# A linear-attention and expert kernel: ids and biases later, first weights copied to a fixed buffer

## The chip, the cores and the metric

The kernel runs on one core of a Trainium2 chip. The core has a matrix engine (TensorE, PE in the profile, with its weight loads shown as PEld), VectorE (DVE), ScalarE (ACT), GpSimd (POOL) and SyncE (SP), which here only issues DMA transfers. Each engine works through its own list of instructions in order; semaphores hold an instruction until what it needs is there. The metric is the device time of one execution in microseconds, the median of the runs.

## The reference

Two stages in a row, cut to what matters:

```python
# 1. gated linear attention, B=4, H=8, S=768, D=48
scale = np.minimum(mag, 0.999) / (mag + 1e-06)      # mag = |a|, a = a_re + i a_im
for t in range(S):
    S_re, S_im = (ar * S_re - ai * S_im + kv, ar * S_im + ai * S_re)   # kv = k_t outer v_t
    y[:, :, t] = q_t @ S_re
# 2. a mixture of experts on x = y as (3072 tokens, 384), top 1 of E=8, F=1024
logits = x @ w_gate + modality_bias[modality_id]
e_idx = argmax(logits); gate_w = softmax(logits)[e_idx]
out[mask] = gate_w[mask, None] * (relu(x[mask] @ w1[e]) @ w2[e])       # for each expert e
```

The ids (`modality_id`) and the bias table are needed only for the logits of the second stage.

## The kernel before

The attention is done in 24 *units* of 128 time steps by 1 batch, two units to a *pair* (x = 0 to 11). For a pair, `load_a`, `load_qk` and `load_v` fetch the inputs, `logs` and `quotients` turn the gates into logarithms and angles (L367 squares on ACT, L368 their sum on DVE, L369 and L370 products and signs, L373 logarithm, L394 and L395 on DVE again), `moduli` and `fractions` sum them along time with matmuls, `waves` takes sine and cosine, and `unit` does the rest: L513 and L520 scale and rotate q and k on DVE, L528 transposes on PE, then the products (L538, L548, L575, L582), the state (L560, L562, L567, L568, with the decay that goes out to memory and back through L425 and L430), and L596, which gives the token's row and its logits at once. The first pair is treated in two halves. All input loads are issued by SP, in one order.

The second stage first chooses experts (`route`) and scatters each token's row to a slot in memory (L718, POOL). The kernel is written for tokens that use two of the eight experts: `weights` loads the w1 and w2 of these two into slots 0 and 1 (`w1s` takes over the buffers of `ab`, `w2s` those of `cs`). Thirteen expert tiles follow, seven early ones (`start_e`, `slot_e`) whose tokens come from the first 16 units, and six late ones; all have 256 tokens but the last, which has 128. A tile is: load of x (L899, SP), 6 transposes (L911), copy (L917, ACT), up in two halves of 12 matmuls (L939) each followed by a relu (L946, ACT), down in two blocks of 8 matmuls (L953), scaling (L961, L963) and a scatter to the output (L968). Which of the two slots a tile uses is known only when the kernel runs: it is read from `slot` into a register of PE (`number`, L876), and the weights are addressed through it.

The order of instructions on PE, ACT, DVE and SP is not written by hand: `Plan.solve` runs through time with an estimated duration for each step and gives a free engine the ready step with the lowest rank. `land` and `queue` are its estimates of a DMA's latency and of its time in the DMA queue; a step without `queue` is taken to land without standing behind other loads. It also gives out buffers: `PM` (2 of them) holds `pm` in the units. The engines then keep this order, whatever the real times are.

Of the kernel before, what the change touches and what calls it, by code (L numbers as in the profile page):

```python
# [12 lines left out]
BF16 = mybir.dt.bfloat16  # L13
# [5 lines left out]
ET = mybir.EngineType  # L19
# [156 lines left out]
class Kernel:  # L176
# [432 lines left out]
    def setup(self):  # L609

        P, nc = self.P, self.nc
        r = self.rp = self.pool("rp", 2)
        nM = self.m_bias.shape[0]
        mb = r.tile([128, nM, E_], F32, name="mb", bufs=1)
        ids = r.tile([128, self.G, self.B, 2], I32, name="ids", bufs=1)

        def loads():
            for u in range(2):
                nc.sync.dma_start(out=self.sel[u * HALF:u * HALF + self.D, :, self.D:], in_=self.w_gate.rearrange("(j u d) e -> u d j e", u=2, d=self.D)[u])
            nc.sync.dma_start(out=mb[:].rearrange("p m e -> p (m e)"), in_=self.m_bias.rearrange("m e -> (m e)")[None, :].broadcast_to([128, nM * E_]))  # L620
            for b in range(self.B):
                nc.sync.dma_start(out=ids[:, :, b], in_=self.ids[b * self.G * L:(b + 1) * self.G * L].bitcast(I32).rearrange("(g p w) -> p g w", p=L, w=2))

        P.step(SP, 0.7, loads, writes=[("sel",), ("ids",)], rank=30.0, land=3.0)

        def biases():
            is_m = r.tile([128, self.NU], F32, name="is_m", bufs=1)
            one = r.tile([128, self.NU, E_], F32, name="one_m", bufs=1)
            for m in range(nM):
                nc.vector.tensor_scalar(is_m[:], ids[:].rearrange("p g b w -> p (g b) w")[:, :, 0], float(m), None, Alu.is_equal)  # L630
# [10 lines left out]
    def route(self, m0, m1, rank):  # L641

        P, nc, r = self.P, self.nc, self.rp
        n, M = m1 - m0, 8
# [23 lines left out]
            box.update(sh=sh, oneh=oneh, acc=acc[:])  # L668
            self.acc.append(acc[:])

        P.step(DVE, 1.3, choose, reads=[("bias",), *[("lg", m) for m in range(m0, m1)], *([("acc",)] if m0 else [])], writes=[("acc",), ("oneh", key), ("sh", key)], rank=rank)

        def ranks():
            before = self.acc[self.batches.index((m0, m1)) - 1] if m0 else None
# [36 lines left out]
            box["pos"] = t("pos_i", dt=I32, bufs=3)  # L711
            nc.vector.tensor_copy(box["pos"], pos)

        P.step(DVE, 0.8, slots, reads=[("rank", key), ("place",), ("oneh", key)], writes=[("pos", key)], rank=rank + 2)
        for m in range(m0, m1):
            def scatter(m=m):
                lo = self.raw["LO", "all"]
# [18 lines left out]
    def guess(self, rank):  # L736

        P, nc = self.P, self.nc
        P.tile(("cnt", 0), "bank")
        P.step(PE, 0.2, lambda: self.count("cnt", 0), reads=[("acc",)], writes=[("cnt", 0)], rank=rank)  # L740
        self.ab = ab = self.small("ab", 2, E_)
        row = self.small("place_row", 2, E_)
        self.place = self.keep.tile([128, 2 * E_], F32, name="place")
        io8 = self.iota[0:1, 0:E_]

        def choose():
            used, nth, nab, two, tw = self.small("used", E_), self.small("nth", E_), self.small("nab", E_), self.small("two", 2, E_), self.small("tw", 2)
# [12 lines left out]
            nc.vector.scalar_tensor_tensor(row[:, 1], ab[:, 1], float(self.N - 1), row[:, 1], Alu.mult, Alu.add)  # L760

        P.step(DVE, 2.0, choose, reads=[("cnt", 0)], writes=[("first",), ("prow",)], rank=rank + 1)
# [22 lines left out]
    def early(self, rank):  # L785

        P, nc, N = self.P, self.nc, self.N
        P.tile(("cnt", "e"), "bank")
        P.step(PE, 0.2, lambda: self.count("cnt", "e"), reads=[("acc",)], writes=[("cnt", "e")], rank=rank)
        self.eA = self.small("eA", 1)  # L790

        def places():
            c2, c, is_b, st = self.small("c2e", 2), self.small("ce", 1), self.small("isb_e", NE), self.small("st_e", NE)
            self.counts_of_two("e", c2)
            f = self.floor_shift("fe", c2[:, 0:1], 8)
            nc.vector.tensor_scalar(self.eA[:], f[:], float(NE), None, Alu.min)
# [9 lines left out]
        P.step(DVE, 2.0, places, reads=[("cnt", "e")], writes=[("early",)], rank=rank + 1)  # L806

    def final(self, rank):

# [32 lines left out]
        P.step(DVE, 3.2, places, reads=[("cnt", "f"), ("early",)], writes=[("final",)], rank=rank + 1)  # L842

        def masks(ps):
            at = self.rp.tile([128, NF_, 2], F32, name="at_f", bufs=1)
# [32 lines left out]
    def expert(self, n, rank):  # L878
# [34 lines left out]
        def xT():  # L913
            return self.buf(("xT", n), KD, m * 128, dt=BF16)
# [13 lines left out]
                nc.vector.tensor_tensor(self.meta[:, n, 0:m].bitcast(I32), meta.bitcast(I32), self.pen[:, i, 0:m], Alu.bitwise_or)  # L928

        P.step(DVE, 0.15, kept, reads=[("xg", n), *([] if early else [("pen",)])], writes=[("meta", n)], rank=rank + 1.5)  # L930
        for q in range(2):
            def up(q=q):
                if q == 0:
                    box["slot"] = bass.ds(self.number(slot[0:1, i:i + 1], ET.PE, 1), 1)
                hp = self.pair((f"h{q}", n), 2, m * 128)
                for f in range(4):
                    ff = 4 * q + f
                    for k in range(KD):
                        nc.tensor.matmul(hp[:, f // 2, f % 2], self.w1s[:, box["slot"], k, ff * 128:(ff + 1) * 128].rearrange("p s f -> p (s f)"), xT()[:, k], start=k == 0, stop=k == KD - 1)  # L939

            P.step(PE, 0.65 * m, up, reads=[("xT", n), known, ("w1", 0), ("w1", 1)], writes=[(f"h{q}", n)], rank=rank + 2)
            eng = ACT

            def relu(q=q):
                to = hT()[:, 4 * q:4 * q + 4].rearrange("p (b f) n -> p b f n", b=2)
                nc.scalar.activation(to, self.pair((f"h{q}", n), 2, m * 128), Act.Relu)  # L946

            P.step(eng, 0.45 * m + 0.05, relu, reads=[(f"h{q}", n)], writes=[("hT", n, q)], rank=rank + 2)
        for s in range(m):
            def down(s=s):  # L950
                yp = self.pair(("yps", n), Dt)[:, s]
                for f in range(NF):
                    nc.tensor.matmul(yp, hT()[:, f, s * 128:(s + 1) * 128], self.w2s[:, box["slot"], f].rearrange("p s d -> p (s d)"), start=f == 0, stop=f == NF - 1)  # L953
# [232 lines left out]
```

## Time and profile before

| | |
|---|---|
| median of 3 runs | 392.07 us (389.61 to 392.19) |
| the profiled execution | 391.36 us, span 389.7 us |
| PE busy | 310.8 us (80%) |
| ACT busy | 246.4 us (63%) |
| DVE busy | 215.1 us (55%) |
| POOL busy | 63.7 us (16%) |
| L939 on PE | 312 matmuls, 70.7 us |
| L953 on PE | 200 matmuls, 36.8 us |

All durations in the profile are from the one profiled execution. A busy row has, in this order, the line in the code, engine, operation, output and inputs by the program's names, shape and count; behind the bar the busy time in us, the mean of one in ns, and behind the next bar the idle time just before it with what ended it. In rows in order of time the first two numbers are start and duration in us, and a bracket shows the idle time before. `PEldq` and `SPq` are the instruction queues of PE and SP; FUSED_REGOPS is an instruction that computes an address in registers.

### The profile page before, as it was taken

Reading aid. Unit: us, or ns where it says so; the run is one execution under the profiler, and the core shown is the slowest. Engines: PE = TensorE matmul, PEld = TensorE weight load, DVE = VectorE, ACT = ScalarE, POOL = GpSimd, SP = SyncE. Lnnn points to the kernel's source line nnn. Section 1 sums busy time; section 2 is a strip of 40 time slices with the busy share of each in tenths; the row PEclk is TensorE's granted clock in tenths of the full one; section 3 lists DMA queues with packets and bytes.
Section 4 is the critical chain, followed back from the end, with each engine's and each line's share of the span. In section 5 each row is a group of like instructions: output and inputs, shape, how many; then the busy total and the mean of one; then the engine's idle time right before and its main releaser. Section 6 shows DMA issues by size and latency. Waiting matters only on the chain.

```text
span 389.7 us, 14470 instructions
## 1 busy us (share of the span) xinstructions
PE 310.8 (80%) x5990; PEld 210.1 (54%) x5990; DVE 215.1 (55%) x431; ACT 246.4 (63%) x297; POOL 63.7 (16%) x93
## 2 busy tenths in 40 slices
PE   0006483788999899999996979899999999999980
PEld 0002362665767668686776667785645454454530
DVE  1026586669998999999997699830351010000000
ACT  4007694999999999898996797752524333434310
POOL 8000000000000027005002210030253141222220
PEclk9999998699999999999999799999999999999986
DMA  8986335446696727774698249430132130311110
GB/s 164 206 99 110 69 72 82 83 85 112 113 177 103 121 55 155 140 133 108 116 172 142 70 75 207 70 87 2 62 105 82 41 116 15 115 40 53 40 45 7
DMA packets 153965, 37.50 MB, mean 96 GB/s; under 512 B 145938, under 2 KB 151592, under 8 KB 153896
## 3 DMA queue, kind: packets, MB, share of 16 engines
q1 hardware_dynamic: 148264, 26.26, 37.6%
q0 software_dynamic: 5632, 10.25, 10.2%
q8 instruction: 52, 0.85, 0.9%
q14 instruction: 17, 0.14, 0.1%
HBM read 32.47 MB, written 7.33 MB: 102 GB/s over the span
## 4 chain that ended last, share of the span: by engine, by line
PE 54%; issue 14%; DVE 11%; ACT 7%; SPq 6%; DMA 3%; POOL 2%; POOLq 0%; DVEq 0%; ACTq 0%
PE ps L939 11%; PE ps L953 6%; PE ps L582 5%; PE ps L548 5%; PE ps L458 5%; PE ps L538 5%; PE ps L528 4%; PE ps L410 3%; PE ps L575 3%; PE ps L596 3%; POOL out_dram L968 2%; DVE qk L520 2%; PE ps L463 2%; ACT qt L532 2%; DVE cs L474 1%
## 5 line engine op out<-in xcount | busy, mean ns | idle before, releaser
L939 PE MATMUL ps<-neg,ab 128*128 128x256 bf16 (+1 forms) x312 | 70.7, 265 | 3.7 <-issue 2.1
L946 ACT ACTIVATE qi<-ps 128x1024 bf16<-128x1024 f32 (+1 forms) x26 | 25.8, 990 | 69.5 <-PE ps L939 56.0
L718 POOL DMA_INDIRECT x_slots<-lo,pos_i x24 | 27.5, 1147 | 183.5 <-DVE lg L605 146.0
L939 PEld LDWEIGHTS <-ab 128*128 x312 | 29.7, 96 | 43.8 <-issue 10.7
L410 PE MATMUL ps<-lm,half 128*128 128x384 f32 x48 | 23.6, 577 | 31.1 <-DVE lm L394 29.6
L528 PE MATMUL ps<-ident,qk 64*128 64x64 f32 x768 | 33.5, 238 | 14.9 <-DVE qk L520 13.2
L520 DVE TENSOR_TENSOR qk<-cs,qi 128x1536 f32<-128x1536 f32 x24 | 41.7, 1751 | 3.0 <-ACT cs L487 2.9
L963 DVE TENSOR_SCALAR lm<-ps,meta 128x384 f32<-128x384 f32 x12 | 7.4, 616 | 63.1 <-PE ps L953 63.1
L968 POOL DMA_INDIRECT out_dram<-lm,meta x25 | 24.6, 985 | 89.5 <-ACT lm L961 84.4
L528 PEld LDWEIGHTS ps<-ident,qk 64*128 64x128 f32 x768 | 28.7, 149 | 18.6 <-DVE qk L520 8.5
L953 PE MATMUL ps<-cs,qi 128*128 x200 | 36.8, 333 | 0.5 <-ACT qi L946 0.5
L313 ACT ACT_TABLE_LOAD x27 | 34.6, 1283 | 1.4 <-PEq L1170 0.9
L373 ACT ACTIVATE sq<-sq 128x1536 f32<-128x1536 f32 (+1 forms) x13 | 18.2, 1398 | 21.0 <-DVE sq L368 21.0
L548 PE MATMUL ps<-v,qk 64*64 64x48 f32 x1408 | 29.3, 228 | 2.2 <-ACT kt L532 1.4
L538 PE MATMUL ps<-qt,kt 128*64 128x64 f32 x768 | 28.1, 225 | 2.9 <-issue 1.6
L548 PEld LDWEIGHTS ps<-v,qk 64*64 64x64 f32 x1408 | 26.3, 142 | 4.4 <-ACT kt L532 1.6
L410 PEld LDWEIGHTS ps<-lm,half 128*128 128x128 f32 x48 | 9.0, 216 | 35.3 <-issue 32.1
L538 PEld LDWEIGHTS ps<-qt,kt 128*64 128x64 f32 x768 | 24.7, 138 | 5.3 <-ACT qt L532 2.3
L458 PE MATMUL ps<-tan,turn 128*128 128x384 f32 x48 | 22.1, 543 | 6.3 <-ACT tan L441 4.8
L953 PEld LDWEIGHTS <-qi 128*128 128x128 bf16 x200 | 19.3, 99 | 13.5 <-ACT qi L946 1.9
L532 ACT COPY kt<-ps 128x1024 f32<-128x1024 f32 x24 | 24.4, 1016 | 1.9 <-PE ps L528 1.6
L532 ACT COPY qt<-ps 128x1024 f32<-128x1024 f32 x24 | 24.6, 1027 | 1.1 <-PE ps L528 1.1
(166 smaller groups left out, 509.2 us busy)
## 6 DMA issues: line engine op xcount, KB each, us to landing
ab<-in_a_re_dram SPq DMA_DIRECT2D x24, 192.0 KB
ab<-in_a_im_dram SPq DMA_DIRECT2D x24, 192.0 KB
qi<-in_k_dram SPq DMA_DIRECT2D x24, 192.0 KB
qi<-in_q_dram SPq DMA_DIRECT2D x24, 192.0 KB
v<-in_v_dram SPq DMA_DIRECT2D x24, 192.0 KB
tan<-x_slots SPq DMA_DIRECT2D x12, 194.0 KB
ab<-in_moe_w_dram POOLq DMA_DIRECT2D x2, 768.0 KB, 8.1
cs<-in_moe_w_dram POOLq DMA_DIRECT2D x2, 768.0 KB, 12.0
```

The costliest lines, as they stand in the source:

```text
L313: self.P.step(ACT, 1.3, lambda: nc.scalar.preload_act_table_set(which), writes=[("table",)], rank=self.rank_table)
L410: nc.tensor.matmul(ls[:, i], self.half[:], lm, start=True, stop=False)
L458: nc.tensor.matmul(us[:, i], self.turn[:], self.buf(("tan", x), 2, H, D)[:, i], start=True, stop=False)
L520: nc.vector.tensor_tensor(self.buf(("QK", w), 4 * H, HALF)[:, :, 0:D], wave, twice, Alu.mult)
L528: nc.tensor.transpose(tp[:, s, h], QK()[rows_[s], k, h].rearrange("t c d -> t (c d)"), self.ident[rows_[s], rows_[s]])
L532: P.step(ACT, 0.91, lambda name=name, to=to: nc.scalar.copy(self.buf((to, w), 2, H, HALF), self.pair((name, w), H, HALF)), reads=[(name, w ...
L538: nc.tensor.matmul(wp[rows_[s], h, :], KT[:, s, h], QT[:, s, h], start=True, stop=True)
L548: nc.tensor.matmul(up[c * HALF:(c + 1) * HALF, s, h], QK()[rows_[s], 0, h, c], V[rows_[s], h, 0:D], start=True, stop=True)
L718: put = nc.gpsimd.indirect_dma_start(out=self.xs, out_offset=bass.IndirectOffsetOnAxis(ap=box["pos"][:, m - m0:m - m0 + 1].bitcast(U32), a ...
L939: nc.tensor.matmul(hp[:, f // 2, f % 2], self.w1s[:, box["slot"], k, ff * 128:(ff + 1) * 128].rearrange("p s f -> p (s f)"), xT()[:, k], s ...
L953: nc.tensor.matmul(yp, hT()[:, f, s * 128:(s + 1) * 128], self.w2s[:, box["slot"], f].rearrange("p s d -> p (s d)"), start=f == 0, stop=f ...
L968: sc = nc.gpsimd.indirect_dma_start(out=self.out, out_offset=bass.IndirectOffsetOnAxis(ap=self.meta[:, n, s, 1:2], axis=0), in_=self.buf(( ...
```

## The change

It has four parts. The ids and the bias table are loaded in a step of their own, with a condition, a later rank and a queue time for the planner; the gate weights are loaded in another. The step that makes the biases gets a later rank. For every expert tile a new DVE step (`picked`) reads the slot into a register of DVE and copies the tile's w1 (128 partitions by 3072 bf16) to a buffer of kind `PM`, from which up's matmuls load their weights without a register; the register on PE is now read in down. And some DVE durations that the planner uses are larger.

```diff
-        def loads():
+        def gate():
             for u in range(2):
                 nc.sync.dma_start(out=self.sel[...], in_=self.w_gate...)
+
+        P.step(SP, 0.2, gate, writes=[("sel",)], rank=6.0, land=2.5, queue=0.6)
+
+        def loads():
             nc.sync.dma_start(out=mb..., in_=self.m_bias...)
             for b in range(self.B):
                 nc.sync.dma_start(out=ids[:, :, b], in_=self.ids...)
-        P.step(SP, 0.7, loads, writes=[("sel",), ("ids",)], rank=30.0, land=3.0)
+        P.step(SP, 0.5, loads, reads=[("asked", 2, 1)], writes=[("ids",)], rank=60.0, land=4.0, queue=6.0)
...
-        P.step(DVE, 1.2, biases, reads=[("ids",)], writes=[("bias",)], rank=60.0)
+        P.step(DVE, 1.4, biases, reads=[("ids",)], writes=[("bias",)], rank=90.0)
...
-        P.step(DVE, 1.3, choose, reads=[("bias",), ...
+        P.step(DVE, 1.6, choose, reads=[("bias",), ...
...
-        for name, kind in (("xg", "TAN"), ("xT", "NEG"), ("hT", "QI"), ("y", "LM")):
+        for name, kind in (("xg", "TAN"), ("xT", "NEG"), ("hT", "QI"), ("y", "LM"), ("w1t", "PM")):
             P.tile((name, n), kind)
...
+        def w1t():
+            return self.buf(("w1t", n), KD, self.F, dt=BF16)
+
+        def picked():
+            at = bass.ds(self.number(slot[0:1, i:i + 1], ET.DVE, 1), 1)
+            nc.vector.tensor_copy(w1t()[:, None], self.w1s[:, at])
+
+        P.step(DVE, 0.95, picked, reads=[known, ("w1", 0), ("w1", 1)], writes=[("w1t", n)], rank=rank + 1.5)
         for q in range(2):
             def up(q=q):
-                if q == 0:
-                    box["slot"] = bass.ds(self.number(slot[0:1, i:i + 1], ET.PE, 1), 1)
                 hp = self.pair((f"h{q}", n), 2, m * 128)
...
-                        nc.tensor.matmul(hp[:, f // 2, f % 2], self.w1s[:, box["slot"], k, ff * 128:(ff + 1) * 128]..., xT()[:, k], ...)
-            P.step(PE, 0.65 * m, up, reads=[("xT", n), known, ("w1", 0), ("w1", 1)], writes=[(f"h{q}", n)], rank=rank + 2)
+                        nc.tensor.matmul(hp[:, f // 2, f % 2], w1t()[:, k, ff * 128:(ff + 1) * 128], xT()[:, k], ...)
+            P.step(PE, 0.69 * m, up, reads=[("xT", n), ("w1t", n)], writes=[(f"h{q}", n)], rank=rank + 2)
...
             def down(s=s):
+                if s == 0:
+                    box["slot"] = bass.ds(self.number(slot[0:1, i:i + 1], ET.PE, 1), 1)
```

Three places show how the lists of instructions move; from the changed `up` on, the line numbers are up to 12 higher.

The start of DVE's list. `is_m`, `one_m` and `bias` belong to the bias step. Before:

```order
L369 TENSOR_TENSOR tan_60<-ab 128x384
L370 TENSOR_SCALAR neg_62<-ab 128x384
L368 TENSOR_TENSOR sq_59<-sq_59 128x384
L630 TENSOR_SCALAR is_m<-ids 128x24
L632 TENSOR_TENSOR bias<-is_m,mb 128x192
L630 TENSOR_SCALAR is_m<-ids 128x24
L632 TENSOR_TENSOR one_m<-is_m,mb 128x192
L634 TENSOR_TENSOR bias<-bias,one_m 128x192
L369 TENSOR_TENSOR tan_60<-ab 128x384
L370 TENSOR_SCALAR neg_62<-ab 128x384
L368 TENSOR_TENSOR sq_59<-sq_59 128x384
```

And now:

```order
L369 TENSOR_TENSOR tan_60<-ab 128x384
L370 TENSOR_SCALAR neg_62<-ab 128x384
L368 TENSOR_TENSOR sq_59<-sq_59 128x384
L369 TENSOR_TENSOR tan_60<-ab 128x384
L370 TENSOR_SCALAR neg_62<-ab 128x384
L394 TENSOR_SCALAR lm_64<-sq_59 128x384
L368 TENSOR_TENSOR sq_59<-sq_59 128x384
```

The five bias instructions are gone from between the two halves of the first pair. They now stand thirty places later in DVE's list, behind the second unit's L562. SP's list keeps the place of the ids among the opening loads; only the gate weights move ahead of two loads of v.

PE's list at the first expert tile, where `ab` holds w1 and `neg` the tile's transposed x. Before:

```order
L876 TENSOR_LOAD slot_e
L939 ISA
L939 LDWEIGHTS ab
L939 ISA
L939 MATMUL ps<-neg_62,ab 128x256
L939 ISA
L939 LDWEIGHTS ab
L939 ISA
L939 MATMUL ps<-neg_62,ab 128x256
```

And now, with `pm` as the fixed buffer:

```order
L949 LDWEIGHTS pm_70
L949 MATMUL ps<-neg_62,pm_70 128x256
L949 LDWEIGHTS pm_70
L949 MATMUL ps<-neg_62,pm_70 128x256
L949 LDWEIGHTS pm_70
L949 MATMUL ps<-neg_62,pm_70 128x256
```

Of four instructions for each matmul, the two ISA (register) instructions are gone, and the slot's load with them.

DVE's list at the first two copies, among the last units (`mid`, `w` and `lg` are the units' own):

```order
L560 TENSOR_TENSOR mid_90<-st_92,ps 128x384
L880 TENSOR_LOAD slot_e
L940 ISA
L940 COPY pm_70<-ab 128x3072
L930 COPY meta<-tan_60 128x4
L560 TENSOR_TENSOR mid_89<-st_93,ps 128x384
L880 TENSOR_LOAD slot_e
L940 ISA
L940 COPY pm_71<-ab 128x3072
L930 COPY meta<-tan_61 128x4
L541 TENSOR_TENSOR w_87<-ps,mask_128 128x512
```

Before, the same rows stood there without the slot loads and the copies, and all later copies are new rows of the same kind, one for each tile.

More of the change, by code (lines that the diff above doesn't have):

```diff
@@ L669, in choose @@
             self.acc.append(acc[:])
-        P.step(DVE, 1.3, choose, reads=[("bias",), *[("lg", m) for m in range(m0, m1)], *([("acc",)] if m0 else [])], writes=[("acc",), ("oneh", key), ("sh", key)], rank=rank)
+        P.step(DVE, 1.6, choose, reads=[("bias",), *[("lg", m) for m in range(m0, m1)], *([("acc",)] if m0 else [])], writes=[("acc",), ("oneh", key), ("sh", key)], rank=rank)
         def ranks():
@@ L712, in slots @@
             nc.vector.tensor_copy(box["pos"], pos)
-        P.step(DVE, 0.8, slots, reads=[("rank", key), ("place",), ("oneh", key)], writes=[("pos", key)], rank=rank + 2)
+        P.step(DVE, 0.95, slots, reads=[("rank", key), ("place",), ("oneh", key)], writes=[("pos", key)], rank=rank + 2)
         for m in range(m0, m1):
@@ L760, in choose @@
             nc.vector.scalar_tensor_tensor(row[:, 1], ab[:, 1], float(self.N - 1), row[:, 1], Alu.mult, Alu.add)
-        P.step(DVE, 2.0, choose, reads=[("cnt", 0)], writes=[("first",), ("prow",)], rank=rank + 1)
+        P.step(DVE, 2.6, choose, reads=[("cnt", 0)], writes=[("first",), ("prow",)], rank=rank + 1)
         self.spread("place", lambda: row[:].rearrange("o a e -> o (a e)"), 2 * E_, [("prow",)], rank + 2, lambda ps: nc.vector.tensor_copy(self.place[:], ps), [("place",)])
@@ L804, in places @@
             nc.vector.tensor_copy(self.slot_e[:], is_b[:])
-        P.step(DVE, 2.0, places, reads=[("cnt", "e")], writes=[("early",)], rank=rank + 1)
+        P.step(DVE, 2.8, places, reads=[("cnt", "e")], writes=[("early",)], rank=rank + 1)
     def final(self, rank):
@@ L840, in places @@
             nc.vector.tensor_copy(self.others[:], left[:])
-        P.step(DVE, 3.2, places, reads=[("cnt", "f"), ("early",)], writes=[("final",)], rank=rank + 1)
+        P.step(DVE, 5.0, places, reads=[("cnt", "f"), ("early",)], writes=[("final",)], rank=rank + 1)
         def masks(ps):
@@ L938, in up @@
                     for k in range(KD):
-                        nc.tensor.matmul(hp[:, f // 2, f % 2], self.w1s[:, box["slot"], k, ff * 128:(ff + 1) * 128].rearrange("p s f -> p (s f)"), xT()[:, k], start=k == 0, stop=k == KD - 1)
-            P.step(PE, 0.65 * m, up, reads=[("xT", n), known, ("w1", 0), ("w1", 1)], writes=[(f"h{q}", n)], rank=rank + 2)
+                        nc.tensor.matmul(hp[:, f // 2, f % 2], w1t()[:, k, ff * 128:(ff + 1) * 128], xT()[:, k], start=k == 0, stop=k == KD - 1)
+            P.step(PE, 0.69 * m, up, reads=[("xT", n), ("w1t", n)], writes=[(f"h{q}", n)], rank=rank + 2)
             eng = ACT
```

## The prediction

> **What bounds the kernel now.** I read the busy slices first, then each end of the span by itself, because the slices show three regimes.
>
> ```profile
> PE   0006483788999899999996979899999999999980
> DVE  1026586669998999999997699830351010000000
> ACT  4007694999999999898996797752524333434310
> 0.00:20.00 20.00, 0.00 (x0) 0.00 (x0) 1.42 (x3) 4.62 (x6) 8.10 (x40) 1.00 1.01 186
> 320.00:340.00 20.00, 19.60 (x105) 9.40 (x103) 1.53 (x4) 7.57 (x9) 4.62 (x5) 1.00 0.24 78
> ```
>
> A slice is 9.7 us. Until about 80 us the engines have gaps; from 80 to 260 us PE, DVE and ACT are all full; after that PE alone is full. The last two rows are from the table of stages (PE, weight loads, DVE, ACT, POOL, then granted clock, DMA share, GB/s): in the first 20 us DVE works 1.42 us while the DMA engines are saturated at 186 GB/s, and in a late stage PE works 19.60 of 20 us while DVE works 1.53. So the first and the last stage have one limit each, and the change touches both.
>
> The start, from DVE's and ACT's waits up to 60 us and the timeline:
>
> ```profile
> DVE is_m L630 <- DMA ids<-in_moe_modality_id_dram: 20.1, 1, 20.1
> ACT sq L373 <- DVE sq L368: 21.0, 2, 20.4
> 5.76 0.56 DVE L368 TENSOR_TENSOR sq<-sq 128x384 f32<-128x384 f32 x1
> 7.10 0.83 ACT L367 ACTIVATE sq<-ab 128x768 f32<-128x768 f32 x1
> 21.90 2.40 SPq L622 DMA_DIRECT2D ids<-in_moe_modality_id_dram  x4
> 26.40 0.18 DVE L630 TENSOR_SCALAR is_m<-ids 128x24 f32<-128x24 int32 x1 [20.08 <-DMA ids<-in_moe_modality_id_dram]
> 28.62 0.55 DVE L368 TENSOR_TENSOR sq<-sq 128x384 f32<-128x384 f32 x1
> 45.02 1.97 PE L528 MATMUL ps<-ident,qk 64*128 64x64 f32 x32 [5.00 <-DVE qk L520]
> ```
>
> DVE finishes the first half's sum of squares at 6.3 us and then stands at the bias step until the ids land at 26.4, because the ids are the last of the opening loads on SP's queue. The second half's squares were ready at 7.9 us, but its sum (L368) runs at 28.62; ACT's logarithm, and through it the first unit at 45.02, hang on that.
>
> The tail, from the chain that ended last, stage rows of single lines (PE busy and count, then the weight loads), the groups, and the waits from 285 to 370 us:
>
> ```profile
> 298.30 2.80 PE ps L953 x16
> 315.81 2.71 PE ps L953 x16
> 333.21 2.73 PE ps L953 x16
> 298.00:316.00 18.00, 10.95 (x48) 4.58 (x48) 1.00 0.23 72
> 298.00:316.00 18.00, 6.08 (x35) 3.33 (x36) 1.00 0.23 72
> L939 PE MATMUL ps<-neg,ab 128*128 128x128 bf16 x24 | 5.2, 216 | 0.6 <-issue 0.2
> L911 PE MATMUL ps<-identb,tan 128*128 128x128 bf16 x75 | 5.3, 219 | 0.0
> DVE lm L963 <- PE ps L953: 48.8, 8, 10.9
> ACT qi L946 <- PE ps L939: 39.6, 16, 3.4
> ```
>
> Two expert tiles take 17.4 us (from one x16 block to the one two blocks on: 298.30, 315.81, 333.21). The two stage rows are L939 and then L953. A pair holds 48 up matmuls at 10.95/48 = 0.228 us, 32 down matmuls at 6.08/35 = 0.174, and 12 transposes at 5.3/75 = 0.071: 10.9 + 5.6 + 0.9 = 17.4. PE's own work is the whole period; DVE and ACT wait for it.
>
> **The change, part by part.**
>
> *The up matmuls lose their register instructions.* Each matmul of L939 stands between two of these:
>
> ```profile
> L939 PEldq FUSED_REGOPS  x624: 46/55/60, 262.2 to 376.1; - x156
> 297.37 0.76 PEld L911 LDWEIGHTS <-tan 128*128 128x128 bf16 x12
> 297.47 0.83 PE L911 MATMUL ps<-identb,tan 128*128 128x128 bf16 x12
> 327.41 2.62 PE ps L953 x16
> L946 ACT ACTIVATE qi<-ps 128x1024 bf16<-128x1024 f32 x24 | 24.6, 1023 | 63.6 <-PE ps L939 50.1 <-issue 13.5
> ```
>
> Four instructions a matmul at some 55 ns make 0.22 us, which is L939's pace, and it doesn't matter how many columns it streams: the last tile's form with 128 columns still takes 5.2/24 = 0.217. So the instruction stream sets the pace, not the array. After the change it is a load and a matmul, like L911 (two instructions, 128 columns, 0.071); L953 has three and 384 columns (0.174). The 256-column pace is not in the trace. Upper bound 0.174, as if it cost what L953 costs; lower bound L953's best block by columns, 2.62/16 x 256/384 = 0.109. Midway between L911 and L953 lies 0.122. I take 0.115, since L953 still carries a register instruction. A pair then takes 48 x 0.115 + 5.6 + 0.9 = 12.0 us. I add 0.3 for a wait that is now late next: the second tile's down must wait for its relu (1.02 us, L946), and only 0.83 us of transposes stand between. Saved: 17.4 - 12.3 = 5.1 a pair, and 30.6 for the six pairs; the last tile saves 24 x (0.217 - 0.071) = 3.5. **Tail: 34 us**, with bounds 2.3 a pair (17 in all) and 5.4 (36).
>
> The Trainium skill, TensorE: Matmul & The Clock Gate, section Back-to-back issue gap, puts the warm gap for N columns at N/2.4 + 2.5 ns, an estimate of 109 ns here; by it the sum would be some 2 us lower.
>
> *The slot load on PE* moves from up to down: 0.3 us either way.
>
> ```profile
> L876 PEldq TENSOR_LOAD <-slot_e x7: 297/307/492, 261.6 to 317.9; - x7
> L395 DVE TENSOR_TENSOR tan<-tan,sq 128x768 f32<-128x768 f32 x11 | 10.5, 955 | 0.0
> L394 DVE TENSOR_SCALAR lm<-sq 128x768 f32<-128x768 f32 x11 | 6.3, 575 | 0.0
> DVE mid L560 <- PE ps L548: 4.3, 3, 2.1
> 231.08 0.78 POOL L871 DMA_DIRECT2D ab<-in_moe_w_dram  x1 [14.20 <-ACT kt L532]
> DMA to landing us min/median/max: 8.1/10.0/12.0
> 286.88 0.96 POOL L718 DMA_INDIRECT x_slots<-lo,pos_i  x1 [0.30 <-issue]
> ```
>
> *The copies on DVE* (13, each 128x3072 bf16, with a slot load of 0.3). By bytes L394 gives 2 x 0.575 = 1.15 us, by elements L395 gives 4 x 0.955 = 3.8; I take 1.5, nearer to the row with one input. DVE works 1.5 of 20 us in the tail, and a copy has a tile's whole period to spare because there are two buffers (the copy for tile n+2 may start once up n is done). That hides all but the first two, which stand among the last units, ahead of L560. There DVE already waits for PE, 4.3 us between 240 and 285 us, so I charge **1 us** (0 to 3). The second w1 load was issued at 231.08 and lands within 12 us, ten before the first copy's place near 253 us, so the copy's new wait holds nothing up. The late tiles need the last scatter, issued at 286.88; that falls earlier with everything ahead of it, and at 6.2 us a tile the seven early ones still last longer.
>
> *The bias step leaves DVE's head.* The second L368 can run once its squares are there (7.93) and five short instructions are done, at about 8.4 instead of 28.6: 20.2 us earlier, and the units with it, as their inputs don't hold them. Twelve loads of 192 KB, the gates' and the first q and k, are 2.36 MB, at 186 GB/s 12.7 us; q and k are first used at 34.71 - 20.2 = 14.5. Some of it comes back:
>
> ```profile
> ab<-in_a_re_dram SPq DMA_DIRECT2D x24, 192.0 KB
> 24.41 0.48 SPq L325 DMA_DIRECT2D ab<-in_a_re_dram  x1
> 34.71 1.82 DVE L513 TENSOR_TENSOR qi<-qi,pm 128x768 f32<-128x768 f32 x2
> 34.94 1.33 SPq L430 DMA_DIRECT2D mt<-m_scr  x2
> 50.49 0.55 DVE L568 TENSOR_TENSOR st<-st,mt 128x384 f32<-128x384 f32 x1
> ```
>
> SP's queue is in the same order here and still reaches the third pair's loads at 24.4. Behind them come the decay's way out and back (L425, L430). L568 will want it at 50.49 - 20.2 = 30.3. With four loads ahead (24.4 to 26.6), the write and its landing behind their 0.79 MB (4.2 us), two more loads and L430's own 1.33, I put it at 33. DVE stands at L568 for 2.7 us with the next half's L395 queued behind. The five bias instructions (1.4 us) now lie among DVE's waits of the second unit; I charge 0.5. **Start: 17 us**, bounds 12 and 20. The middle is full on three engines and only shifts.
>
> *The planner's other costs* reorder neighbours in the units, with no instruction more or less: 0, give or take 2. The split-off gate load has slack (used by L596 at 58 us).
>
> **Sum.** The profiled execution took 391.36 us (span 389.7), 0.7 below the median of 392.07. 391.4 - 34 - 17 + 1 = **341 us**. The forecast's own range, with all bounds at their one end or the other: 391.4 - 36 - 20 = 335 to 391.4 - 17 - 12 + 3 = 365.
>
> **The rivals.**
>
> *The start gains little* (12%). If SP's queue and the decay's loop set the pace of the first units, DVE's wait moves to L568 and the next loads, and 5 us, my estimate, are left of 17: 353. For it: SP issues without a gap until 24.4, and L430 waits for a landing. Against: one unit's loop costs a few us, not 12.
>
> *The weight load comes out from under the matmul* (5%). Its row:
>
> ```profile
> L953 PEld LDWEIGHTS <-qi x200: 95/98/147, 273.6 to 378.2; 128*128 128x128 bf16 x100
> ```
>
> If a full load of 0.098 can't run under a matmul, up costs 0.098 + 0.115 = 0.213 a matmul, saves 0.015 x 288 = 4 us, and the time is 391.4 - 4 - 3 - 17 + 1 = 370. Against: L953 has such a load each time and paces at 0.174, which would leave 0.076 for 384 columns, hardly more than L911's 0.071 for 128. The Trainium skill, TensorE: Matmul & The Clock Gate, Part 3 (The mechanism), has that rule: a load overlaps running matmuls only where the row group differs, and here all groups are the same. By that rule the time is the 370; the trace disagrees.
>
> *A new wait in the tail* (5%). If relu, POOL's scatter or the x loads end later than I think, a pair takes 14.5 instead of 12.3: 13 us less gained, 354.
>
> *Slower: the copies become the bound* (3%). All tiles' copies go through one DVE. At c us each a pair can't be shorter than 2c; to lose the 16 us of the start over six pairs it must exceed 17.4 + 16/6 = 20.1, so it decides from c = 10. At 11 the time is 391.4 - 16 + 6 x 4.6 = 403. Against: L395, the slowest row, gives 3.8.
>
> *It doesn't do what it says* (2%): PE's pace is held by something other than the register instructions and DVE waits elsewhere; within 1% of 391.
>
> **Chances and range.** Forecast 73%, the rivals as given. Eight in ten or more lie between 333 and 365: the forecast with its bounds and 2 us of reordering below, the start's and the tail's rivals, but not 370 and beyond. A measurement here can't tell less than about 1% from nothing. Faster by more than that: 73 + 12 + 5 + 5 = 95%; within it 2%; slower 3%.
>
> **What would show it.** DVE's wait of 20 us gone and the first transposes (L528) at 26 to 29 us; a DVE wait at L568 of 2 to 3 us for the mt load; the up matmuls at 0.11 to 0.12 us each and a pair of tiles at 12 to 13 us; the copies at 1 to 2 us, and nobody waiting for them. Wrong: up above 0.17, PE waiting for the copies, or the start's gain gone by 100 us.

## The result, and the profile after

| | before | after |
|---|---|---|
| median of 4 runs | 392.13 us (389.61 to 392.31) | 347.37 us (346.28 to 348.71) |
| the profiled execution | 391.36 us, span 389.7 | 348.71 us, span 347.0 |
| PE busy | 310.8 us | 272.4 us |
| DVE busy | 215.1 us | 226.7 us |

The ratio is 0.887, with a 95% interval of 0.882 to 0.892. The forecast was 341 us, with a range of 333 to 365. The total hides two misses of opposite sign: the tail gave 39 us where 34 were forecast, and the start gave 4 to 9 where 17 were.

**The tail.** The groups of the page's kind, with the two forms of up kept apart (busy time, mean ns of one, idle time before it), in the changed kernel; up is L949 here, its relu L956, down L965, the copy L940:

```profile
L949 PE MATMUL ps<-neg,pm 128*128 128x256 bf16 x288 | 33.8, 273 | 0.0
L949 PEld LDWEIGHTS <-pm 128*128 128x128 bf16 x312 | 29.3, 98 | 4.7
L940 DVE COPY pm<-ab 128x3072 bf16 x13 | 12.4, 958 | 8.4 <-PE ps L949 7.7 <-DVE meta L932 0.4 <-PE ps L738 0.3
L949 PE MATMUL ps<-neg,pm 128*128 128x128 bf16 x24 | 1.5, 219 | 0.0
```

All up matmuls took 70.7 us of PE before; now they take 33.8 + 1.5 = 35.3. A 256-column one takes 33.8/288 = 0.117 us and a 128-column one 1.5/24 = 0.063, so that the time follows the columns now, which it didn't before (0.228 and 0.217). The weight loads take 98 ns each (96 before) and lie under the matmuls. A copy takes 0.96 us, and in its row it is the copies that wait for PE to be done with their buffer, not PE for them.

The timeline of PE, one pair of expert tiles of the changed kernel from one block of 16 down matmuls to the same block of the next pair (start, duration):

```profile
302.22 2.76 PE L965 MATMUL ps<-cs,qi 128*128 x16
304.82 1.47 PE L949 MATMUL ps<-neg,pm 128*128 128x256 bf16 x12
306.13 0.83 PE L915 MATMUL ps<-identb,tan 128*128 128x128 bf16 x12
306.80 2.88 PE L965 MATMUL ps<-cs,qi 128*128 x16
309.51 4.09 PE L949 MATMUL ps<-neg,pm 128*128 128x256 bf16 x36
313.44 2.76 PE L965 MATMUL ps<-cs,qi 128*128 x16
```

A pair takes 313.44 - 302.22 = 11.22 us; it took 17.4. From start to start, the 36 up matmuls take 3.93 us or 0.109 each, the first 16 down matmuls 2.60 or 0.163 each, the 12 transposes 0.67 or 0.056 each. The durations beside them are 0.13 to 0.17 us longer than these distances: by the profile, whose ends of matmuls are modelled, a block ends that long after the next one has started. The first up matmul and the last down block of the kernel before, and the last down block now:

```profile
262.50 2.92 PE L939 MATMUL ps<-neg,ab 128*128 128x256 bf16 x12 [0.20 <-issue]
376.37 2.72 PE L953 MATMUL ps<-cs,qi 128*128 x8
334.03 1.46 PE L965 MATMUL ps<-cs,qi 128*128 x8 [0.57 <-ACT qi L956]
```

From the first up to the end of the last down the tail took 116.6 us before (262.50 to 379.1) and takes 77.3 now (258.20 to 335.5).

**The start.** The waits of the changed kernel in its first 60 us (us in total, times, longest):

```profile
PE ps L528 <- DVE qk L520: 20.1, 1, 20.1
DVE qk L520 <- ACT cs L487: 16.4, 1, 16.4
ACT cs L487 <- DMA cr<-cs: 15.4, 2, 15.2
```

DVE's wait of 20.1 us for the ids is gone from this view, and a chain of three that ends in a DMA stands in its place. The timeline shows how it comes about (a bracket is the idle time before):

```profile
7.97 0.56 DVE L368 TENSOR_TENSOR sq<-sq 128x384 f32<-128x384 f32 x1
19.77 0.55 DVE L474 TENSOR_TENSOR cs<-cs,ps 128x384 f32<-128x384 f32 x1
21.24 2.26 SPq L626 DMA_DIRECT2D ids<-in_moe_modality_id_dram  x4
33.83 0.84 SPq L430 DMA_DIRECT2D mt<-m_scr  x2
34.77 1.50 SPq L477 DMA_DIRECT2D cr<-cs  x2
36.59 0.52 ACT L487 ACTIVATE cs<-cs 128x384 f32<-128x384 f32 x1 [15.22 <-DMA cr<-cs]
39.05 1.97 PE L528 MATMUL ps<-ident,qk 64*128 64x64 f32 x32 [20.05 <-DVE qk L520]
...
258.20 1.49 PE L949 MATMUL ps<-neg,pm 128*128 128x256 bf16 x12
```

The second sum of squares (L368) runs at 7.97, as the forecast said. The angles of both halves are ready at 20.3 (the last end of L474). One row of each half's angles has to be kept for the next block of time steps, and this document calls it the carry: L477 copies it from `cs` to `cr` with a DMA. L487 then takes the sine *in place*, on the same `cs`, and so must wait until that copy has read its row. The two copies stand in SP's queue behind the ids, eight gate loads of the third and fourth pair and the first pair's decay, and they are issued at 34.77, 14.5 us after the second row was there. Of the 13.5 us from the ids (21.24) to these copies, SP's rows hold about 10 us of issuing; most of the rest is time in which SP waits for the decay's way out to land. In the timeline of the kernel before the sine of the first half reads:

```profile
42.56 0.52 ACT L487 ACTIVATE cs<-cs 128x384 f32<-128x384 f32 x1 [0.17 <-DMA cr<-cs]
```

There DVE came 20 us later, SP had worked off its queue in that time, and the sine waited 0.2 us. The same queue was there, hidden behind a longer wait. The first transposes (L528) start at 39.05 instead of 45.02, 6.0 us earlier, and the first up matmul at 258.20 instead of 262.50, 4.3 us earlier.

### The profile page after: what moved, and what is told of

It reads as the page before. It is cut to its first block, busy times and chain, and to the rows that moved or that the text cites. A ratio compares the mean times of both kernels' runs of the same rounds, so it can differ in the third digit from the quotient of the medians.

```text
span 347.0 us, 13899 instructions
## 1 busy us (share of the span) xinstructions
PE 272.4 (79%) x5990; PEld 208.3 (60%) x5990; DVE 226.7 (65%) x444; ACT 246.4 (71%) x297; POOL 69.2 (20%) x93
## 4 chain that ended last, share of the span: by engine, by line
PE 35%; issue 16%; ACT 13%; DVE 11%; SPq 10%; POOL 7%; DMA 5%; POOLq 0%; DVEq 0%; ACTq 0%
POOL out_dram L980 6%; PE ps L582 5%; PE ps L548 4%; PE ps L410 4%; PE ps L538 3%; PE ps L458 3%; PE ps L528 3%; PE ps L575 3%; PE ps L596 3%; ACT kt L532 2%; DMA m_scr<-pm 2%; PE ps L463 2%; ACT qt L532 2%; SPq L325 2%; SPq L337 2%
## 5 line engine op out<-in xcount | busy, mean ns | idle before, releaser
L722 POOL DMA_INDIRECT x_slots<-lo,pos_i x24 | 30.3, 1264 | 169.2 <-ACT sq L367 126.4
L528 PE MATMUL ps<-ident,qk 64*128 64x64 f32 x768 | 33.0, 235 | 29.0 <-DVE qk L520 28.1
L528 PEld LDWEIGHTS ps<-ident,qk 64*128 64x128 f32 x768 | 28.4, 147 | 32.5 <-issue 21.5
L956 ACT ACTIVATE qi<-ps 128x1024 bf16<-128x1024 f32 (+1 forms) x26 | 25.8, 991 | 29.2 <-PE ps L949 20.6
L980 POOL DMA_INDIRECT out_dram<-lm,meta x25 | 26.6, 1063 | 51.3 <-ACT lm L973 46.3
L965 PE MATMUL ps<-cs,qi 128*128 x200 | 35.4, 326 | 1.5 <-ACT qi L956 1.0
L949 PE MATMUL ps<-neg,pm 128*128 128x256 bf16 (+1 forms) x312 | 35.3, 269 | 0.0
L949 PEld LDWEIGHTS <-pm 128*128 128x128 bf16 x312 | 29.3, 98 | 4.7
L965 PEld LDWEIGHTS <-qi 128*128 128x128 bf16 x200 | 19.2, 97 | 13.8 <-ACT qi L956 1.9
L513 DVE TENSOR_TENSOR qi<-qi,pm 128x768 f32<-128x768 f32 x24 | 22.8, 953 | 3.5 <-ACT pm L417 3.5
L487 ACT ACTIVATE cs<-cs 128x768 f32<-128x768 f32 (+1 forms) x13 | 10.2, 786 | 18.2 <-DMA cr<-cs 18.2
```

The lines of the kernel that those rows point to most:

```text
L528: nc.tensor.transpose(tp[:, s, h], QK()[rows_[s], k, h].rearrange("t c d -> t (c d)"), self.ident[rows_[s], rows_[s]])
L722: put = nc.gpsimd.indirect_dma_start(out=self.xs, out_offset=bass.IndirectOffsetOnAxis(ap=box["pos"][:, m - m0:m - m0 + 1].bitcast(U32), a ...
L949: nc.tensor.matmul(hp[:, f // 2, f % 2], w1t()[:, k, ff * 128:(ff + 1) * 128], xT()[:, k], start=k == 0, stop=k == KD - 1)
L980: sc = nc.gpsimd.indirect_dma_start(out=self.out, out_offset=bass.IndirectOffsetOnAxis(ap=self.meta[:, n, s, 1:2], axis=0), in_=self.buf(( ...
```

## The experiments

All changes are made on the changed kernel, and the planner's larger DVE durations stay in all of them. Where runs of different groups are compared, it is by their ratio to the kernel before, which ran beside each group.

### The two parts alone

*Start alone*: up addresses its weights through the register as before.

```diff
-        P.step(DVE, 0.95, picked, reads=[known, ("w1", 0), ("w1", 1)], writes=[("w1t", n)], rank=rank + 1.5)
...
-    nc.tensor.matmul(..., w1t()[:, k, ff * 128:(ff + 1) * 128], ...)
+    nc.tensor.matmul(..., self.w1s[:, box["slot"], k, ff * 128:(ff + 1) * 128]..., ...)
```

> Only the ids, biases and planner part of the change; up is addressed through the register as before, and nothing is copied. Theory (the start's gain is eaten, since ACT's second sine of the first pair must wait until the carry copy, far back in SP's queue, has read its rows): first transposes L528 near 39 us with the second sine's wait for the carry of 15 us in the trace, and a time of 385 to 389 us. Rival, the prediction's own term (the start is worth 17 us): 373 to 378 us. Rival that the ids part is worth nothing at the end: 391 to 393 us.

386.9 us, ratio 0.989 (0.985 to 0.993). In its timeline:

```profile
36.92 0.52 ACT L487 ACTIVATE cs<-cs 128x384 f32<-128x384 f32 x1 [15.47 <-DMA cr<-cs]
39.38 1.97 PE L528 MATMUL ps<-ident,qk 64*128 64x64 f32 x32 [20.30 <-DVE qk L520]
256.46 2.92 PE L943 MATMUL ps<-neg,ab 128*128 128x256 bf16 x12 [0.31 <-issue]
```

The wait for the carry is there without any copy of weights, and the first up comes 6.0 us earlier than before (262.50). The start part as it was made is worth 4 us by the medians and 6.1 by the spans of the profiled executions (389.7 to 383.6), not 17.

*Copy alone*: the step `loads` and the rank of the bias step as before.

> Only the copy of the tile's first weights; ids and biases are loaded and used as before. Theory read from the two traces (the tail is shorter by about 39 us): 352 to 355 us, with the first L528 near 45 us and a pair of tiles at 11.2 us. Rival, the prediction's size of it (34 us less, 1 us more for the first copies): 358 us.

354.87 us, ratio 0.909 (0.903 to 0.916), span 353.1. DVE's wait for the ids is back in the view of waits:

```profile
DVE is_m L630 <- DMA ids<-in_moe_modality_id_dram: 20.3, 1, 20.3
```

The copy is worth 36 us by the medians and 36.6 by the spans. That is 3 less than the tail's 39, mostly since the first up matmul comes later:

```profile
264.18 1.48 PE L945 MATMUL ps<-neg,pm 128*128 128x256 bf16 x12
```

In this timeline it is 1.7 us later than before (262.50), with the first units where they were; the same 1.7 lie between the start alone (256.46) and the changed kernel (258.20), and so the 6.0 us of the start become 4.3 at the first up. The spans of the four profiled executions add up: the start takes off 6.1 with the old up (389.7 to 383.6) and 6.1 with the new one (353.1 to 347.0). By the ratios it is 1.1% (4 us) with the old up and 2.2% (9 us) with the new one. Executions of one kernel differ by 2 us and more, so 4 to 9 us is as fine as these runs tell, and the 1.7 us rest on single executions.

### What holds the start: the carry on another queue

```diff
-                P.step(SP, 0.1, lambda i=i: nc.sync.dma_start(out=self.crs[x % 2]..., in_=...)
+                own = x == 0
+                P.step(POOL if own else SP, 1.0 if own else 0.1, lambda i=i, own=own: (nc.gpsimd if own else nc.sync).dma_start(out=self.crs[x % 2]..., in_=...)
```

> The changed kernel, but the first pair's two carry copies are issued by POOL instead of standing in SP's queue. Theory (the in-place sine waits for that copy, and nothing else holds the first unit): the second sine of the first pair at 24 to 25 us instead of 36.6, first L528 at about 27 us, DVE then waits 2 to 4 us for the decay at L568, and the time is 335 to 340 us. Rival (SP's queue and the decay's loop set the pace of the first units anyway): L528 comes early but the first up matmul moves by less than 3 us, time 344 to 348 us.

337.04 us (336.66 to 337.12), ratio 0.863 (0.858 to 0.867): 10 us faster than the changed kernel, from the engine that issues two small copies. Its timeline (lines behind L477 are one higher):

```profile
18.86 0.79 POOL L478 DMA_DIRECT2D cr<-cs  x1 [8.73 <-DVE cs L474]
21.50 0.52 ACT L488 ACTIVATE cs<-cs 128x384 f32<-128x384 f32 x1 [0.16 <-DMA cr<-cs]
23.96 1.97 PE L529 MATMUL ps<-ident,qk 64*128 64x64 f32 x32 [4.99 <-DVE qk L521]
33.28 0.56 DVE L569 TENSOR_TENSOR st<-st,mt 128x384 f32<-128x384 f32 x1 [3.83 <-DMA mt<-m_scr]
55.71 1.53 PE L549 MATMUL ps<-v,qk 64*64 64x48 f32 x48
246.99 1.48 PE L950 MATMUL ps<-neg,pm 128*128 128x256 bf16 x12
```

The first half's sine no longer waits, and the first transposes come at 23.96, 15 us earlier than after the change. DVE now waits 3.83 us for the decay at the state update: the wait that the forecast had named (2.7 us at L568), which the changed kernel doesn't show because the carry stands in front of it. The third unit's update starts at 55.71; in the kernel before it is at 71.79 and after the change at 65.35:

```profile
71.79 1.42 PE L548 MATMUL ps<-v,qk 64*64 64x48 f32 x44
```

```profile
65.35 0.89 PE L548 MATMUL ps<-v,qk 64*64 64x48 f32 x24
```

These are the timelines of before and of after. From the third unit on the distances stay: 16.1 us there and 15.5 at the first up against before, 9.6 and 11.2 against after. With the carry out of the way the start is worth 353.1 - 335.5 = 17.6 us of span against the copy alone.

### The place in the queue, or SP itself

The carry stays on SP, but the order of its queue is changed after the planner is done:

```diff
         P.solve()
+        carry = [s for s in P.order if s["engine"] == SP and s["tiles"] == {("cs", 0)}]
+        late = [P.writer[name] for name in (("mt", 0, 0), ("mt", 0, 1), ("ab", 2, 0), ("ab", 2, 1), ("ab", 3, 0), ("ab", 3, 1), ("ids",))]
...
+        P.order = rest[:at] + late + rest[at:]      # at: right behind the last carry
```

> The changed kernel with another order in SP's queue alone: behind the opening loads first the first pair's way out for the decay and its two carry copies, then the decays, then the third and fourth pair's gate loads, then bias table and ids. Theory (the place in SP's queue is all that held the start): second sine of the first pair at 22 to 24 us, first L528 at 24 to 27 us, no DVE wait over 1 us for the decay, time 332 to 337 us, no worse than with the carry on POOL. Rival (SP itself is too slow, or the delayed gate loads are late next): 338 to 347 us.

337.11 us, ratio 0.861 (0.856 to 0.867), at the upper edge of what the theory gave (337):

```profile
21.11 1.48 SPq L477 DMA_DIRECT2D cr<-cs  x2
23.63 0.94 ACT L487 ACTIVATE cs<-cs 128x384 f32<-128x384 f32 x2 [2.28 <-DMA cr<-cs]
26.09 1.97 PE L528 MATMUL ps<-ident,qk 64*128 64x64 f32 x32 [7.10 <-DVE qk L520]
31.60 0.55 DVE L568 TENSOR_TENSOR st<-st,mt 128x384 f32<-128x384 f32 x1
54.89 1.96 PE L548 MATMUL ps<-v,qk 64*64 64x48 f32 x64
```

The carry is issued at 21.11 instead of 34.77, and the wait for the decay is gone. So it is the place in the queue, not SP as such. That the wait of 3.8 us is gone as well brings nothing more: the third unit is again at 55; a part of the reason shows in the run with both cures below.

*Ids alone moved* behind the carry in SP's queue (the same edit with `("ids",)` alone in the list):

> The changed kernel with one step moved in SP's queue: bias table and ids (five transfers, 3.2 us of issue) from the opening loads to behind the first pair's carry copies. Theory (the carry's place in the queue sets the first unit): the second sine of the first pair comes 3 us earlier, at 33 to 34 us, first L528 at 36 us, and of that 2 to 3 us are kept: 344 to 346 us. Rival (the queue ahead is not what the carry waits for): no change, 347 to 348 us.

346.28 us, ratio 0.884 (0.879 to 0.889), which can't be told from the changed kernel's 0.887. In the timeline, that of a run of 348.36 us, the sine moves by 2 us:

```profile
34.64 0.52 ACT L487 ACTIVATE cs<-cs 128x384 f32<-128x384 f32 x1 [13.32 <-DMA cr<-cs]
```

That is the right direction for the theory, less than the 3 us of issue that were taken out of the queue, and inconclusive for the time.

### Which number of the start part does the work

The copy, and the old step for gates, bias table and ids, with one number more:

```diff
-        P.step(SP, 0.7, loads, writes=[("sel",), ("ids",)], rank=30.0, land=3.0)
+        P.step(SP, 0.7, loads, writes=[("sel",), ("ids",)], rank=30.0, land=3.0, queue=6.0)
```

> The copy, and of the whole start part only one number: the old step for gate weights, biases and ids is kept, with the planner told that it takes 6 us in the DMA queue. Theory (the loads' own split, condition and rank did nothing, since SP issues them at the same place; what helped is that the planner no longer puts the bias step at DVE's head): the first second-half sum L368 at about 8 us, the second sine of the first pair waiting for the carry until 36 to 37 us, and the time of the changed kernel, 346 to 349 us. Rival (the split or the later rank of the loads matter): 351 to 355 us, as with the copy alone.

This run and the next two were made on a chip where the kernel before takes 412.5 us, so only their ratios are used. It is 0.886 (0.881 to 0.891), the changed kernel's 0.887. Its timeline has the changed kernel's start:

```profile
8.41 0.56 DVE L368 TENSOR_TENSOR sq<-sq 128x384 f32<-128x384 f32 x1 [0.37 <-ACT sq L367]
37.12 0.52 ACT L487 ACTIVATE cs<-cs 128x384 f32<-128x384 f32 x1 [15.31 <-DMA cr<-cs]
```

The ids are not loaded later in the changed kernel (SP issues them at 21.24, before at 21.90), and they needn't be. To tell the planner when they land, so that it puts the bias step behind the work of the first units, is enough for all that the start part gained. Whether the later rank of the bias step alone would have been enough too was not tried.

### Both cures of the start together

The carry on POOL, and in SP's queue the decays, then the gate loads, then the ids:

> The carry copies of the first pair issued by POOL and, in SP's queue, the first pair's decays ahead of the third and fourth pair's gate loads, with bias table and ids last. Theory (with the carry on POOL the next wait is DVE's 3.8 us for the decay at the state update, which this order takes away): that wait under 0.5 us, first transposes at 24 us, time 332 to 335 us. Rival (the start's later units are bound elsewhere by then): 336 to 338 us, no better than either change alone.

> The changed kernel with the first pair's carry copies on POOL once more, beside the version with the reordered queue: 336 to 338 us.

Ratios 0.861 (0.856 to 0.865) for both cures and 0.862 (0.856 to 0.868) for the carry on POOL alone, run beside it. The times of this chip are not those that were expected; as a share of the 391 us of the kernel before, the theory's 332 to 335 would be 0.849 to 0.857, and the rival's 336 to 338 is 0.859 to 0.864. The comparison goes with the rival: both cures are no better than one, though the interval still touches the theory's upper edge. DVE's wait for the decay (L569) is gone with both cures, as the theory said, and the first transposes start at 24.66, but the second pair's sine waits in its place:

```profile
49.75 0.84 ACT L488 ACTIVATE cs<-cs 128x768 f32<-128x768 f32 x1 [3.87 <-DMA cr<-cs]
50.63 3.43 DVE L521 TENSOR_TENSOR qk<-cs,qi 128x1536 f32<-128x1536 f32 x2 [2.85 <-ACT cs L488]
```

This is the carry once more, that of the second pair, which still goes through SP's queue; with the carry first the same sine waits 3.04 us, with the first pair's carry on POOL 1.00. So the units that come earlier run into the same kind of wait one pair later. No run moved this copy, so what its cure would give is not shown.

### What the copy costs

Up reads slot 0 at a fixed address, so that the choice between the two experts is left out of it, and there is no copy:

```diff
-    nc.tensor.matmul(..., w1t()[:, k, ff * 128:(ff + 1) * 128], ...)
+    nc.tensor.matmul(..., self.w1s[:, 0, k, ff * 128:(ff + 1) * 128], ...)
```

> The changed kernel without the copy: up takes its weights straight from slot 0 at a fixed address, so the choice between the two experts is left out in up. Up's matmuls then keep the form they have after the change, at 0.117 us each, with no copy and no register. Theory (the copies are hidden beside PE): 346 to 349 us, the same as the changed kernel. Rival (the copies cost time among the last units or in the tail): faster by their cost, 3 us for 0.25 us a tile, 343 to 345 us, and up to 335 us if all 12.4 us of copies lie on the path.

347.36 us (347.17 to 347.48), ratio 0.889 (0.885 to 0.894), against 347.37. Up's group is the changed kernel's to the tenth:

```profile
L941 PE MATMUL ps<-neg,ab 128*128 128x256 bf16 x288 | 33.8, 273 | 0.0
```

The first up starts at 257.92 in this execution, 0.3 us earlier than in the changed kernel's, so the copies don't explain the 1.7 us by which it comes later; where these come from was not followed. The 12.4 us of copies on DVE cost nothing that can be measured, and it is the fixed address that makes up fast, not the buffer that the weights come from.

### What one register costs

The weights stay fixed, and the moving operand is addressed through the register:

```diff
-    nc.tensor.matmul(..., w1t()[:, k, ff * 128:(ff + 1) * 128], xT()[:, k], ...)
+    nc.tensor.matmul(..., w1t()[:, k, ff * 128:(ff + 1) * 128], xT()[:, box["slot"]]..., ...)
```

> The changed kernel, weights still from the copy at a fixed address, but up's moving operand (the tile's x) is addressed through the slot register, one of x's first two chunks in place of all three: that part of the product is left out of the computation. Each up matmul then has one register instruction, as down's has, three instructions in all. Theory (PE's instruction stream at about 55 ns each sets the pace where it is longer than the columns): up goes from 0.109 to 0.165 us a matmul, a pair of tiles from 11.2 to 13.9 us, the last tile 2.4 us more, time 364 to 367 us. Rival (the register instruction runs beside the columns, only the two of a weight address hurt): 346 to 350 us.

355.12 us, ratio 0.911 (0.905 to 0.917): 8 us slower than the changed kernel by the medians and 9 by the ratios, between the expectations. PE's timeline in one pair and in the last tile:

```profile
284.66 2.87 PE L965 MATMUL ps<-cs,qi 128*128 x16
287.44 3.20 PE L951 MATMUL ps<-neg,pm 128*128 x24
291.00 1.85 PE L951 MATMUL ps<-neg,pm 128*128 x12 [0.36 <-issue]
292.71 2.76 PE L965 MATMUL ps<-cs,qi 128*128 x16
295.31 1.47 PE L951 MATMUL ps<-neg,pm 128*128 x12
296.62 0.83 PE L915 MATMUL ps<-identb,tan 128*128 128x128 bf16 x12
297.29 2.88 PE L965 MATMUL ps<-cs,qi 128*128 x16
337.77 3.24 PE L951 MATMUL ps<-neg,pm 128*128 x24
340.99 1.61 PE L965 MATMUL ps<-cs,qi 128*128 x8
```

A pair takes 12.63 us (284.66 to 297.29). Three quarters of its up matmuls run at (292.71 - 287.44)/36 = 0.146 us, with gaps named "issue", and the last tile's, with 128 columns, at 3.22/24 = 0.134. So one register instruction is enough to make the pace nearly independent of the columns: the instructions set it, as the theory says, but at 0.146 for three and not 0.165, so 55 ns for each of them is not the price. The register is in the moving operand's address here, and was in the weights' before; whether one register costs the same in both was not tried. The other quarter, the 12 behind a down block, keeps 0.109 (295.31 to 296.62), which the theory had not foreseen. The kernel before has a like difference: in its pair from 315.65 to 333.05 the 12 behind a down block take (332.38 - 329.87)/12 = 0.209 each, the other 36 (327.27 - 318.55)/36 = 0.242. That the instructions get ahead while down's longer matmuls run would give this, but no run shows it.

*Down without a register*: on the version with the carry first, DVE copies the second weights too, to a buffer of kind `QK`.

```diff
+        P.step(DVE, 0.95, picked2, reads=[known, ("w2", 0), ("w2", 1)], writes=[("w2t", n)], rank=rank + 1.6)
...
-    nc.tensor.matmul(yp, hT()..., self.w2s[:, box["slot"], f]..., ...)
+    nc.tensor.matmul(yp, hT()..., w2t()[:, f], ...)
```

> The kernel with the carry first in SP's queue, and in addition DVE copies each tile's second weights to a fixed buffer, so that down's matmuls need no register either. Theory (down already runs at its 384 columns, 0.163 us a matmul, and the one register instruction is hidden): the same time as without this copy, within 2 us. Rival (the register instruction costs its 55 ns in down): a pair is 32 times 0.055 or 1.8 us shorter and the time 10 to 11 us less.

336.16 us, ratio 0.859 (0.853 to 0.865), against 337.11 and 0.861 without it: no difference. Its pair of tiles, with down at L971:

```profile
280.59 2.76 PE L971 MATMUL ps<-qk,qi 128*128 128x384 bf16 x16
283.19 1.47 PE L957 MATMUL ps<-neg,pm 128*128 128x256 bf16 x12
```

The 16 down matmuls take 2.60 us without a register too, 0.163 each. With 384 columns one register instruction is hidden; that fits the pace of 0.146 with one, which is less than 0.163.

## Why the prediction was right or wrong, step by step

- **What bounds the two ends**: right. The copy alone took the tail's time off PE, and DVE's wait for the ids hid the first units.
- **Up's pace**: right in kind, and a little too careful in size. Taken was 0.115 with a lower bound of 0.109; from start to start it is 0.109. The term of the tail, 34 us, came out at 39. A pair takes 11.22 where 12.3 were forecast: 48 x 0.006 = 0.3 of that is up, 0.5 is in down and the transposes, and the wait of 0.3 for the relu did not come. The terms of the sum were block durations, and each of them holds the 0.13 to 0.17 us by which its end lies behind the start of the next block; distances from start to start are what adds up. The Trainium skill, TensorE: Matmul & The Clock Gate, section Back-to-back issue gap, gave an estimate of 109 ns, and the trace agrees (3.93/36 = 0.109). That section of the Trainium skill gives the formula for an isolated matmul and about 81 ns for 128 columns in a stream of loads and matmuls; in such a stream here the transposes keep the formula's pace, at 0.056.
- **The rival of the exposed weight load**: refuted, as forecast. Loads of 98 ns lie under matmuls that follow each other at 0.109. The rule of the Trainium skill, TensorE: Matmul & The Clock Gate, Part 3 (The mechanism), by which a load overlaps only where the row group differs, does not hold here; the same section also lets a load into a background weight buffer go ahead, which would fit, but the trace doesn't show the buffers. In the forecast's own terms this rival adds up to 391.4 - 4 - 3 - 17 + 1 = 368, not 370.
- **The copies, 1.5 us each and 1 us on the path**: 0.96 us each, and on the path 0.3 us at the first up, which single executions can't tell from nothing. "Nobody waiting for them" is what the row of L940 and the run without them show.
- **The start, 17 us**: wrong. The step that failed is "20.2 us earlier, and the units with it, as their inputs don't hold them". L368 did move by 20.6 us. But of the things that the first unit needs, the forecast looked at the loads of q and k and at the decay, and not at the sine that may not overwrite its row before the carry copy has left. It had SP's queue in hand up to 35 us and placed the decay in it, and the carry stands right behind the decay of the second half. In the trace of before this wait is 0.2 us long, because the wait for the ids covered it.
- **The rival "the start gains little"**: right in its result (4 to 9 us of 17 left, where it had 5) and in naming SP's queue, but it moved the wait to L568, and it had only 12%. The reason against it, "one unit's loop costs a few us, not 12", counted the loop and not the whole queue ahead of it.
- **The wait at L568 of 2.7 us**: right behind the one that covered it; 3.83 us once the carry is on POOL. With that cure the start keeps 17.6 us by the spans, the size of the term. That is in part luck: with the carry first in SP's queue the wait at L568 is gone and the time is the same, and the second pair's sine waits 3.04 us for its own carry there.
- **The planner's other costs, 0 give or take 2**: not tried by themselves, but nothing speaks against the term. The start alone has them, and there the first transposes come 5.6 us earlier (45.02 to 39.38) and the first up 6.0.

The total came out within 2% of the forecast because the two misses, 5 us more in the tail and 8 to 13 us less in the start, partly cancel. That is luck.

## What to carry to other kernels

When a wait at the head of a program is taken away, list for the next instructions not only what they read but also who must have read what they overwrite, and look up where that reader stands in its queue: a wait that shows 0.2 us can be 15 us long once the longer one that covered it is gone. Here matmuls whose weights are addressed through a register were bound by their instructions at 128 and at 256 columns; a copy of the weights to a fixed place, on an engine that is idle, can pay, but only as far as the columns don't already take longer than the instructions, as they did at 384. Sum PE's blocks by the distance from start to start, not by their durations.

## What was not expected of the hardware

- One register instruction takes 46 to 60 ns in the row of L939, but it costs more in the pace: a 128-column matmul of the last tile takes 0.063 us with none (1.5/24, busy time), 0.134 with one (3.22/24, from start to start), and 0.217 with two (5.2/24, busy time). The forecast had explained 0.22 by four instructions of 55 ns; three would then be 0.165, and the run with one register shows 0.146 at 256 columns.
- Fixed-address matmuls ran at 0.056 (128 columns, transposes), 0.109 (256) and 0.163 us (384) from start to start: nearly in proportion to the columns, each with a weight load of its own.
- SP's time to issue counts by itself: the four loads of the ids took it 2.26 us, the two carry copies 1.50. In the changed kernel 13.5 us passed between the ids (21.24) and the carry (34.77), with 18 transfers issued ahead of it; about 10 us of that were issuing.
